# Streamed tiles of an expert kernel at other distances from the loaded tiles, a first column per region, and two capacities raised by 4 and 2

## The chip, the core and the metric

The kernel runs on one core of one Trainium2 chip. The metric is the device time of one execution in microseconds, the median of several runs. A core has five engines with queues of their own: TensorE (PE, matrix products; its loads of stationary blocks are listed as PEld), VectorE (DVE), ScalarE (ACT), GpSimd (POOL) and SyncE (SP, which issues most DMA here). SBUF is the on-chip memory of 128 partitions; the products write to PSUM.

## What is computed

Linear attention with a normalisation, then a two-level mixture of experts over its rows, all in float32:

```python
kv = np.einsum('bhsd,bhse->bhde', k, v)
out = np.einsum('bhsd,bhde->bhse', q, kv)
rms = np.sqrt(np.mean(out * out, axis=-1, keepdims=True) + 1e-06)
x = (out / rms * g_norm)                  # as 4608 rows of 512
g_idx = argmax(x @ w_group); g_w = its softmax
for g in range(4):                        # groups
    e_idx = argmax(x[g_idx == g] @ w_expert[g]); e_w = its softmax
    for e in range(4):                    # experts of the group
        h = np.maximum(x_ge @ w1[g, e], 0.0)       # 512 -> 1024
        out[tok_idx] = (g_w * e_w)[:, None] * (h @ w2[g, e])   # 1024 -> 512
```

## The kernel before

**First phase** (to about 158 us). q, k and v are loaded, the attention and the router's decisions are computed, the rows go to a table in DRAM (scr), and the sixteen experts are ranked by their number of rows. The expert of rank 0 is computed largely in this phase. Its products are in plain f32.

**Second phase** (from 158.58 us). A loop over r = 1 to 15 takes the experts in the order of their rank. Each such pass is called a region here. CAPS[r] is the number of row slots that the region has (rows beyond it go to a loop at the end that runs only when it is needed). For a region, GpSimd gathers the rows (xg), they go through DRAM (xd) and come back turned (xq, xt), and ACT and DVE split them into a rounded part xh and a rest xl, both in float32r, a float32 type for the products. The expert's weights come as four pieces of 1 MB (wr) and are split in the same way into whi and wlo. The results go through DRAM (yd) back to rows, and GpSimd scatters them.

A product is then three: high by high, rest by high, high by rest. That is the helper `three` (lines 306 to 316): for each chunk of the inner dimension, line 310 streams the high part against the loaded whi, line 311 streams the rest against whi, and line 315 streams the high part against wlo (in the code's order of the three). Layer 1 (`layer1`) has 8 output blocks x 4 chunks x 3 = 96 such products, streaming xh and xl; its result goes through `split_h` (lines 284 and 285) into hh and hl. Layer 2 (`layer2_by_feature`) has 4 blocks x 8 chunks x 3 = 96, streaming hh and hl. So a region has 192 products, each with CAPS[r] columns that are streamed and a block of 128 x 128 that is loaded. Only in the last region's layer 2 (`layer2_by_token`) are the roles swapped: hh and hl are loaded, and the weights are streamed in 256 columns.

The places in SBUF: the pool `cp` lies first, then `big` (twelve slots of 8 KB, tag w8, with all whi and wlo), then the tiles of the second phase (pool `mp`), among them xg, xq, xt, xh, xl, yo, hh and hl in this order. The tiles xh, xl, hh and hl are 384 columns wide per chunk (1,536 bytes a partition); a region uses the first CAPS[r] of them.

The order of the second phase is written out by hand (`manual_schedule`): each engine runs its instructions in the order of the code.

Of the kernel before, what the change touches and what calls it, by code (L numbers as in the profile page):

```python
# [9 lines left out]
F32 = mybir.dt.float32  # L10
F32R = mybir.dt.float32r
# [7 lines left out]

CAPS = [384, 364, 354, 330, 326, 312, 302, 300, 292, 290, 284, 274, 268, 264, 260, 256]


GS = [8, 7, 5, 5, 7, 4]
# [32 lines left out]
def tile_linattn_moe(ctx: ExitStack, tc: tile.TileContext, qm, qt, k, v, router, w1, w2, out):  # L58
    nc = tc.nc
    P = 128  # L60
# [16 lines left out]
    KC = DM // P  # L77
    FC = FF // P
# [7 lines left out]
    RW = DM + H  # L86
# [2 lines left out]
    yd = [tc.dram_tile([3 * P, DM], F32, name=f"yd{i}") for i in range(2)]  # L89
    ovt = tc.dram_tile([NBLK, 4], F32, name="ovt")  # L90

    cp = ctx.enter_context(tc.tile_pool(name="cp", bufs=1))
    big = ctx.enter_context(tc.tile_pool(name="big", bufs=BIG))


# [61 lines left out]
    for r in range(NE):  # L157
        nc.gpsimd.memset(caps[:, r:r + 1], float(CAPS[r]))
    blk = cp.tile([P, 36], F32, name="blk")
# [83 lines left out]
    def split_piece(w, p, turned=False):  # L243
        for x, hi, lo in quarter(w, p, turned):
            nc.scalar.copy(out=hi, in_=x)  # L245
            nc.vector.tensor_tensor(out=lo, in0=x, in1=hi.bitcast(F32), op=ALU.subtract)  # L246

    def blocks(cap):
        return [(j, min(P, cap - j * P)) for j in range((cap + P - 1) // P)]

    def gather_rows(xg, rows, idx, src=scr):
        return nc.gpsimd.indirect_dma_start(out=xg[0:rows, 0:RW], out_offset=None, in_=src,  # L252
                                            in_offset=bass.IndirectOffsetOnAxis(ap=idx[0:rows, :], axis=0))
# [20 lines left out]
    def scale_rows(eng, xg, out_=None):  # L274

        x = by_quarter(xg[:, 0:DM])
        out_ = x if out_ is None else by_chunk(out_)
        for h in range(2):
            hs = slice(2 * h, 2 * h + 2)
            d = eng.tensor_tensor(out=out_[:, hs], in0=x[:, hs], in1=factors(xg)[:, h], op=ALU.mult)  # L280
        return d

    def split_h(hh, hl, ps):
        nc.scalar.activation(out=hh, in_=ps, func=AF.Relu)  # L284
        nc.vector.scalar_tensor_tensor(out=hl, in0=ps, scalar=0.0, in1=hh.bitcast(F32), op0=ALU.max, op1=ALU.subtract)  # L285

    def layer1(ps, w1, f, xh, xl):
        cs = slice((f % 4) * P, (f % 4 + 1) * P)
        _, wh, wl = w1[f // 4]
        three(ps, KC, lambda c: wh[:, c, cs], lambda c: wl[:, c, cs], lambda c: xh[:, c, :], lambda c: xl[:, c, :])  # L290
# [846 lines left out]
    with ExitStack() as ph:  # L1137
        mp = ph.enter_context(tc.tile_pool(name="moe", bufs=2))
# [87 lines left out]
        def quarter_rows(x, cap, a):  # L1226
            n = (cap + 31) // 32
            return x[0:32 * n, a * P:(a + 1) * P].rearrange("(b i) f -> i b f", i=32)

        def gather(r):  # L1230
            xg = mp.tile([P, 3, RW], F32, name="xg", bufs=1)
            for j, _ in blocks(CAPS[r]):
                st["gather"] = gather_rows(xg[:, j], P, gidx[:, r, j:j + 1])
            return xg

        def scale(r, g):
            for j, _ in blocks(CAPS[r]):
                scale_rows(nc.gpsimd, g[:, j])

        def put_x(r, g):  # L1240
            for j, rows in blocks(CAPS[r] + -CAPS[r] % 32):
                nc.sync.dma_start(xd[r % 2][j * P:j * P + rows, :], g[0:rows, j, 0:DM])

        def get_x(r):
            n = (CAPS[r] + 31) // 32
            xq = mp.tile([P, 12, P], F32, name="xq", bufs=1)
            for a in range(4):
                nc.sync.dma_start(xq[32 * a:32 * a + 32, 0:n, :], quarter_rows(xd[r % 2], CAPS[r], a))
            return xq, mp.tile([P, KC, 384], F32, name="xt", bufs=1)
# [3 lines left out]
            nc.vector.transpose(out=xt[:, c, 0:32 * n].rearrange("p (b i) -> p b i", i=32),  # L1253
                                in_=xq[:, 0:n, 32 * c:32 * c + 32])

        def parts_x():
            return [mp.tile([P, KC, 384], F32R, name=nm, bufs=1) for nm in ("xh", "xl")]

        def split_x(r, parts, xt, c):

# [5 lines left out]
        def put_y(r, yq):  # L1266
            for a in range(4):
                nc.sync.dma_start(quarter_rows(yd[r % 2], CAPS[r], a), yq[32 * a:32 * a + 32, 0:(CAPS[r] + 31) // 32, :])

        def get_y(r, yq):  # L1270
            yo = mp.tile([P, 3 * DM], F32, name="yo3", tag="yo3").rearrange("p (j f) -> p j f", j=3)
            for j, rows in blocks(CAPS[r]):
                nc.sync.dma_start(yo[0:rows, j], yd[r % 2][j * P:j * P + rows, :])
            return [(yo[:, j], rows, gidx[:, r, j:j + 1]) for j, rows in blocks(CAPS[r])]

        def back(r, yt):

            yo = mp.tile([P, 3 * DM], F32, name="yo3", tag="yo3").rearrange("p (j f) -> p j f", j=3)
            for j, rows in blocks(CAPS[r]):
                tp = ps_t.tile([P, 512], F32, name="tp2", tag="pst")  # L1280
                for d in range(KC):
                    nc.tensor.transpose(tp[0:rows, d * P:(d + 1) * P], yt[:, d, j * P:j * P + rows], ident)
                nc.vector.tensor_copy(out=yo[0:rows, j], in_=tp[0:rows, :])
                scatter_rows(yo[:, j], rows, gidx[:, r, j:j + 1])
                yield
# [46 lines left out]
        nxt = gather(1)  # L1332
# [19 lines left out]
        for i in range(2, 4):  # L1352
            load_next(i)
        nxt = gather(2)
        scale(2, nxt)
        for c in range(KC):
# [8 lines left out]
        for hf in range(2):  # L1365
# [1 line left out]
            for f in range(4):  # L1367
                whole1(ps[:, f * P:(f + 1) * P], w1c[hf][:, :, f * P:(f + 1) * P], xT)
            nc.scalar.activation(out=hT[:, 4 * hf:4 * hf + 4], in_=ps.rearrange("p (f t) -> p f t", f=4), func=AF.Relu)
        cur = parts_x()  # L1370
        for c in range(KC):
            turn_x(1, xq, xt, c)
        for c in range(KC):
# [16 lines left out]
        for r in range(1, NE):  # L1390
            cap = CAPS[r]
            xh, xl = cur
            hh = mp.tile([P, FC, 384], F32R, name="hh", bufs=1)
            hl = mp.tile([P, FC, 384], F32R, name="hl", tag="hl", bufs=1)
            if nxt:
                xq, xt = get_x(r + 1)
            if todo and todo[0] in MOVED:
                put_y(*todo)
            elif todo:
                turns = back(*todo)  # L1400
            for f in range(FC):
                if f in w2_at:
                    split_piece(w2c, w2_at[f], r in MOVED)
                ps = ps_h.tile([P, 512], F32, name="ps")
                layer1(ps[:, 0:cap], w1c, f, xh[:, :, 0:cap], xl[:, :, 0:cap])
                split_h(hh[:, f, 0:cap], hl[:, f, 0:cap], ps[:, 0:cap])
                if r > 1:
                    next(tables, None)
                    next(tables, None)
                elif f < len(psys):  # L1410
                    nc.vector.memset(psys[f][:, DM // 2:384], 0.0)
                if f == 0:
                    nxt2 = gather(r + 2) if r + 2 < NE else None
                if nxt2 and f == 1:
                    scale(r + 2, nxt2)
                if f >= 1:
                    next(turns, None)
                if todo and todo[0] in MOVED and f == 2:
                    results = get_y(*todo)
                if nxt and f in (1, 3):  # L1420
                    load_next((f + 3) // 2)
                if nxt2 and f == 4:
                    put_x(r + 2, nxt2)
                if f >= 5 and results:
                    scatter_rows(*results.pop(0))
                if f == FC - 1 and r + 1 == NE:
                    nc.gpsimd.drain()
            nw1a, nw2a, load_a = weight_loads(eidx[0:1, r + 2:r + 3], mp if r % 2 else None) if nxt2 else (None, None, None)
            cur = parts_x() if nxt else None

            def side(n, total, after):
                if nxt is None:
                    return
                if not after:
                    split_piece(nw1, n)
                    if n < 2:
                        turn_x(r + 1, xq, xt, 2 * n)
                        turn_x(r + 1, xq, xt, 2 * n + 1)
                else:
                    for c in ([0], [1, 2], [3], [])[n]:  # L1440
                        split_x(r + 1, cur, xt, c)
                    if n in (1, 3) and nxt2:
                        load_a(n // 2)

            if r + 1 == NE:
                layer2_by_token(r, w2c, hh, hl, side)
            else:
                todo = layer2_by_feature(r, w2c, hh, hl, side)
            w1c, w2c = nw1, nw2
            nxt, nw1, nw2, load_next = nxt2, nw1a, nw2a, load_a  # L1450
# [3 lines left out]
    with ExitStack() as ph:  # L1454
# [4 lines left out]
        with tc.For_i(0, nv, 1) as it:  # L1459
# [19 lines left out]
            xg = op.tile([P, RW], F32, name="xgo")  # L1479
# [90 lines left out]
```

## Time and profile before

| | us |
|---|---|
| median of 3 runs | 567.9 (567.41 to 568.88) |
| profiled execution | 565.66 |
| its span, first to last instruction | 564.0 |
| PE busy | 543.9 (96%) |
| DVE / ACT / POOL busy | 378.1 / 267.1 / 209.3 |
| mean granted clock of TensorE | 0.991 |

The profile is of one execution. A row of a cut (a stretch of the span) gives its start and end, its length, the busy time of each engine in it with the number of instructions that touch it, the granted clock as a share of 2.4 GHz, and the share of the DMA engines' time with the rate. Products are pipelined: one starts well before the one ahead of it has ended, so what a product costs is the time between starts, not its duration.

### The profile page before, as it was taken

How to read it: one execution, taken by the hardware profiler on the slowest of the kernel's cores; microseconds unless marked ns; L12 is line 12 of the kernel's file. 1: busy time of each engine (PE TensorE's matmuls, PEld its weight loads, DVE VectorE, ACT ScalarE, POOL GpSimd, SP SyncE). 2: the span in 40 equal slices, each digit the busy share in tenths (PEclk: the TensorE clock that was granted, in tenths of full speed). 3: DMA queues.
4: the chain of work that ended last, by engine and by line, in shares of the span. 5: the costliest groups of instructions: out<-in, count | busy, mean ns of one | idle time of the engine just before them, and what ended most of it. 6: DMA issues, size and time to landing. Idle time of an engine off the chain costs nothing.

```text
span 564.0 us, 11522 instructions
## 1 busy us (share of the span) xinstructions
PE 543.9 (96%) x4323; PEld 522.6 (93%) x4323; DVE 378.1 (67%) x782; ACT 267.1 (47%) x530; POOL 209.3 (37%) x278
## 2 busy tenths in 40 slices
PE   8999978699899999999999999999999999999995
PEld 3899868588899999999999999999999999999995
DVE  4247888773456796776767676777767686868750
ACT  0377754622444443544444544454546455546540
POOL 5024342144352342533453524344525334433121
PEclk9999998899999999999999999999999999999998
DMA  8999999486889999999998999999999999989940
GB/s 286 388 407 388 370 355 405 126 316 229 281 318 299 283 311 261 274 307 283 309 293 288 281 291 261 320 278 332 313 300 294 292 309 315 319 254 331 271 144 34
DMA packets 78890, 165.21 MB, mean 293 GB/s; under 512 B 8084, under 2 KB 47332, under 8 KB 67824
## 3 DMA queue, kind: packets, MB, share of 16 engines
q1 hardware_dynamic: 70862, 142.29, 78.7%
q0 software_dynamic: 7824, 22.11, 13.1%
q8 instruction: 35, 0.57, 0.4%
q10 hardware_dynamic: 146, 0.04, 0.1%
q14 instruction: 23, 0.19, 0.1%
HBM read 126.38 MB, written 38.55 MB: 292 GB/s over the span
## 4 chain that ended last, share of the span: by engine, by line
PE 69%; DMA 19%; issue 5%; DVE 2%; SPq 2%; ACT 2%; POOL 1%; POOLq 0%; DVEq 0%; ACTq 0%
PE ps L311 8%; PE ps L315 8%; PE ps L310 8%; DMA wr<-in_w_dram 8%; PE psy L311 8%; PE psy L310 8%; PE psy L315 8%; PE ops L515 5%; PE kps L477 3%; PE l L299 3%; PE warm L371 3%; DMA yd<-yq 2%; DMA xd<-xg 2%; DMA xq<-xd 2%; DMA ktail<-in_k_dram 2%
## 5 line engine op out<-in xcount | busy, mean ns | idle before, releaser
L246 DVE TENSOR_TENSOR wlo<-wr,whi 128x1024 fp32r<-128x1024 f32 (+1 forms) x176 | 156.6, 917 | 22.6 <-ACT whi L245 19.1
L311 PE MATMUL ps<-xl,whi 128*128 128x364 f32 (+14 forms) x480 | 144.5, 301 | 0.0
L315 PE MATMUL ps<-xh,wlo 128*128 128x364 f32 (+14 forms) x480 | 144.4, 301 | 0.0
L310 PE MATMUL ps<-xh,whi 128*128 128x364 f32 (+14 forms) x480 | 144.4, 301 | 0.0
L311 PE MATMUL psy<-hl,whi 128*128 128x364 f32 (+13 forms) x448 | 135.5, 302 | 0.0
L315 PE MATMUL psy<-hh,wlo 128*128 128x364 f32 (+13 forms) x448 | 135.4, 302 | 0.0
L310 PE MATMUL psy<-hh,whi 128*128 128x364 f32 (+13 forms) x448 | 135.2, 302 | 0.0
L245 ACT CAST whi<-wr 128x1024 fp32r<-128x1024 f32 (+1 forms) x176 | 128.2, 769 | 1.9 <-DMA wr<-in_w_dram 1.9
L284 ACT ACTIVATE hh<-ps 128x364 fp32r<-128x364 f32 (+14 forms) x120 | 50.4, 420 | 146.8 <-PE ps L315 142.4
L285 DVE SCALAR_TENSOR_TENSOR hl<-ps,hh 128x364 fp32r<-128x364 f32 (+14 forms) x120 | 55.8, 465 | 56.9 <-ACT hh L284 55.2
L310 PEld LDWEIGHTS ps<-xh,whi 128*128 128x128 f32 x480 | 90.8, 189 | 0.0
L315 PEld LDWEIGHTS ps<-xh,wlo 128*128 128x128 f32 x480 | 90.7, 189 | 0.0
L311 PEld LDWEIGHTS ps<-xl,whi 128*128 128x128 f32 x480 | 90.5, 189 | 0.0
L252 POOL DMA_INDIRECT xg<-scr,gall x44 | 52.6, 1196 | 96.2 <-DMA xd<-xg 81.2
L280 POOL TENSOR_TENSOR xg<-xg 128x256 f32<-128x256 f32 x82 | 60.2, 762 | 74.5 <-DMA xg<-scr,gall 74.4
L256 POOL DMA_INDIRECT out_dram<-yo,gall x45 | 51.8, 1150 | 92.8 <-DMA yo<-yd 75.9
L310 PEld LDWEIGHTS psy<-hh,whi 128*128 128x128 f32 x448 | 84.7, 189 | 0.0
L315 PEld LDWEIGHTS psy<-hh,wlo 128*128 128x128 f32 x448 | 84.7, 189 | 0.0
L311 PEld LDWEIGHTS psy<-hl,whi 128*128 128x128 f32 x448 | 84.5, 189 | 0.0
L1262 ACT ACTIVATE xh<-xt,rw 128x364 fp32r<-128x364 f32 (+14 forms) x60 | 32.3, 543 | 48.5 <-DVE xt L1253 45.5
L1315 DVE STREAM_TRANSPOSE yq<-psy 128x320 f32<-128x320 f32 (+3 forms) x56 | 28.5, 510 | 29.9 <-PE psy L315 27.6
L515 PE MATMUL ops<-kvx,m_q 128*128 128x168 f32 x256 | 42.0, 312 | 0.6 <-ACT xr L466 0.6
(250 smaller groups left out, 588.7 us busy)
## 6 DMA issues: line engine op xcount, KB each, us to landing
wr<-in_w_dram SPq DMA_DIRECT2D x64, 1024.0 KB
scr<-xo SPq DMA_DIRECT2D x36, 256.0 KB
m_q<-in_qm_dram SPq DMA_DIRECT2D x8, 1024.0 KB
xd<-xg SPq DMA_DIRECT2D x32, 256.0 KB
m_k<-in_k_dram SPq DMA_DIRECT2D x7, 1024.0 KB
m_v<-in_v_dram SPq DMA_DIRECT2D x7, 1024.0 KB
yo<-yd SPq DMA_DIRECT2D x28, 256.0 KB
xq<-xd SPq DMA_DIRECT2D x20, 160.0 KB
```

Of the source, the lines that this page charges most:

```text
L245: nc.scalar.copy(out=hi, in_=x)
L246: nc.vector.tensor_tensor(out=lo, in0=x, in1=hi.bitcast(F32), op=ALU.subtract)
L252: return nc.gpsimd.indirect_dma_start(out=xg[0:rows, 0:RW], out_offset=None, in_=src, in_offset=bass.IndirectOffsetOnAxis(ap=idx[0:rows, : ...
L256: sc = nc.gpsimd.indirect_dma_start(out=out, out_offset=bass.IndirectOffsetOnAxis(ap=idx[0:rows, :], axis=0), in_=yo[0:rows, :], in_offset ...
L280: d = eng.tensor_tensor(out=out_[:, hs], in0=x[:, hs], in1=factors(xg)[:, h], op=ALU.mult)
L284: nc.scalar.activation(out=hh, in_=ps, func=AF.Relu)
L285: nc.vector.scalar_tensor_tensor(out=hl, in0=ps, scalar=0.0, in1=hh.bitcast(F32), op0=ALU.max, op1=ALU.subtract)
L310: nc.tensor.matmul(ps, lhsT=stat_h(c), rhs=mov_h(c), start=(c == 0), stop=False)
L311: nc.tensor.matmul(ps, lhsT=stat_h(c), rhs=mov_l(c), start=False, stop=False)
L315: nc.tensor.matmul(ps, lhsT=stat_l(d), rhs=mov_h(d), start=False, stop=(d == n - 1))
L515: nc.tensor.matmul(o, lhsT=raw["q", b].rearrange("p j f -> p (j f)")[:, (pr * NJ + j) * P:(pr * NJ + j + 1) * P], rhs=kvx[b % 4][:, pr], s ...
L1262: nc.scalar.activation(out=xh, in_=x, func=AF.Copy, scale=g2[:, 0:1])
```

## The change

Four things change. A tile of 8 float32 columns (32 bytes a partition) named gap is put at the head of `cp`; nothing reads or writes it. The tile xg gets 24 columns (96 bytes) more at its end. A table BEGIN gives for each region the first column that it uses in xh, xl, hh and hl, and a helper `streamed` cuts the tiles accordingly. CAPS[4] goes from 326 to 330 and CAPS[9] from 290 to 292.

```diff
-CAPS = [384, 364, 354, 330, 326, 312, 302, 300, 292, 290, 284, 274, 268, 264, 260, 256]
+CAPS = [384, 364, 354, 330, 330, 312, 302, 300, 292, 292, 284, 274, 268, 264, 260, 256]
+
+BEGIN = [0, 16, 16, 0, 0, 0, 0, 0, 40, 40, 8, 0, 40, 0, 16, 0]
...
     cp = ctx.enter_context(tc.tile_pool(name="cp", bufs=1))
+    cp.tile([P, 8], F32, name="gap")
...
         def gather(r):
-            xg = mp.tile([P, 3, RW], F32, name="xg", bufs=1)
+
+            xg = mp.tile([P, 3 * RW + 24], F32, name="xg", bufs=1)[:, 0:3 * RW].rearrange("p (j f) -> p j f", j=3)
...
-        def parts_x():
-            return [mp.tile([P, KC, 384], F32R, name=nm, bufs=1) for nm in ("xh", "xl")]
+        def streamed(r, nm, n=KC):
+            return mp.tile([P, n, 384], F32R, name=nm, bufs=1)[:, :, BEGIN[r]:BEGIN[r] + CAPS[r]]
+
+        def parts_x(r):
+            return [streamed(r, nm) for nm in ("xh", "xl")]
...
-            hh = mp.tile([P, FC, 384], F32R, name="hh", bufs=1)
-            hl = mp.tile([P, FC, 384], F32R, name="hl", tag="hl", bufs=1)
+            hh, hl = (streamed(r, nm, FC) for nm in ("hh", "hl"))
...
-            cur = parts_x() if nxt else None
+            cur = parts_x(r + 1) if nxt else None
```

The program's instructions stay the same in number and order on every engine.

## Rows read from the trace of the kernel before

**Rows 1.** The page: busy time by engine, and the chain that ended last

```profile
PE 543.9 (96%) x4323; PEld 522.6 (93%) x4323; DVE 378.1 (67%) x782; ACT 267.1 (47%) x530; POOL 209.3 (37%) x278
...
PE 69%; DMA 19%; issue 5%; DVE 2%; SPq 2%; ACT 2%; POOL 1%; POOLq 0%; DVEq 0%; ACTq 0%
```

**Rows 2.** Second phase cut at the starts of regions 1 to 15, busy by engine

```profile
core 0: us, PE busy (x) PEld busy (x) DVE busy (x) ACT busy (x) POOL busy (x), PEclk, DMA share, GB/s
158.58:190.86 32.28, 32.28 (x194) 32.25 (x193) 20.25 (x34) 15.26 (x27) 13.28 (x15) 1.00 1.00 307
190.86:222.85 31.99, 31.99 (x194) 31.99 (x193) 25.29 (x48) 13.69 (x24) 11.43 (x12) 1.00 1.01 285
222.85:252.29 29.44, 29.44 (x193) 29.44 (x193) 21.95 (x48) 13.52 (x24) 11.62 (x14) 1.00 0.95 289
252.29:281.42 29.13, 29.13 (x195) 29.13 (x194) 20.21 (x40) 13.45 (x24) 10.81 (x11) 1.00 1.01 290
281.42:309.15 27.73, 27.73 (x194) 27.73 (x193) 19.41 (x32) 13.34 (x24) 11.42 (x12) 1.00 0.93 292
309.15:336.03 26.88, 26.88 (x195) 26.88 (x193) 19.71 (x32) 13.26 (x24) 12.26 (x12) 1.00 1.02 294
336.03:362.90 26.87, 26.87 (x194) 26.87 (x193) 19.18 (x32) 13.21 (x24) 10.64 (x11) 1.00 0.99 293
362.90:388.31 25.41, 25.41 (x195) 25.41 (x194) 18.52 (x32) 13.15 (x24) 10.49 (x11) 1.00 1.01 300
388.31:414.54 26.23, 26.23 (x194) 26.23 (x193) 19.20 (x32) 13.11 (x24) 11.68 (x12) 1.00 1.02 320
414.54:440.15 25.61, 25.61 (x195) 25.61 (x193) 18.67 (x32) 13.03 (x24) 10.48 (x11) 1.00 0.98 288
440.15:464.68 24.53, 24.53 (x195) 24.53 (x193) 18.39 (x32) 12.95 (x24) 10.62 (x12) 1.00 0.97 281
464.68:488.15 23.47, 23.47 (x195) 23.47 (x194) 18.24 (x32) 12.90 (x24) 11.84 (x12) 1.00 0.98 298
488.15:511.50 23.35, 23.35 (x194) 23.35 (x193) 16.64 (x32) 12.47 (x24) 7.51 (x8) 1.00 0.91 294
511.50:534.56 23.06, 23.06 (x195) 23.06 (x194) 17.37 (x34) 12.77 (x24) 4.54 (x5) 1.00 0.99 305
534.56:557.62 23.06, 23.06 (x194) 22.86 (x192) 9.45 (x15) 7.34 (x15) 5.58 (x6) 1.00 0.36 118
sum 399.04, PE 399.04 PEld 398.81 DVE 282.50 ACT 193.43 POOL 154.22; mean PE 26.60 PEld 26.59 DVE 18.83 ACT 12.90 POOL 10.28
```

**Rows 3.** Chain that ended last, first phase: start, us, what, number of products

```profile
25.10 1.14 PE ops L515 x8
...
33.91 1.14 PE ops L515 x8
...
44.05 1.14 PE ops L515 x8
```

**Rows 4.** Idle time ahead of the instructions that read wr: us, times

```profile
  DMA wr<-in_w_dram: 1.9, 2
```

**Rows 5.** Timeline at region 15's start, DVE and PE: start, us, instruction

```profile
534.19 0.44 DVE L1263 SCALAR_TENSOR_TENSOR xl<-xt,rw,xh 128x256 fp32r<-128x256 f32 x1
...
534.56 0.28 PE L310 MATMUL ps<-xh,whi 128*128 128x256 f32 x1
...
535.75 0.28 PE L311 MATMUL ps<-xl,whi 128*128 128x256 f32 x1
```

**Rows 6.** The first 100 us as one cut, columns as in rows 2

```profile
0.00:100.00 100.00, 92.25 (x1141) 78.79 (x1142) 62.92 (x184) 52.13 (x132) 33.25 (x87) 0.98 1.00 371
```

More of the change, by code (lines that the diff above doesn't have):

```diff
@@ L1369, in tile_linattn_moe @@
             nc.scalar.activation(out=hT[:, 4 * hf:4 * hf + 4], in_=ps.rearrange("p (f t) -> p f t", f=4), func=AF.Relu)
-        cur = parts_x()
+        cur = parts_x(1)
         for c in range(KC):
```

## Prediction

> **What bounds the kernel now.** I read the page first: TensorE (PE) is busy 96% of the span, VectorE (DVE) 67%, and the chain that ended last lies 69% on PE [rows 1]. A share of busy time does not say where, so next comes the second phase cut at the starts of its fifteen regions r = 1 to 15 [rows 2]. In every cut PE is busy for the whole length and the granted clock is 1.00, the 2.4 GHz level. The reader should take from this table only its first two numbers: the 192 products of a region follow each other without a gap, so a region's length over 192 is the time from one product's start to the next. The phase is 399.0 of the 564.0 us, and it is the sum of 2880 such steps.
>
> For bookkeeping I count one streamed column as one period of 2.4 GHz, 0.417 ns. A region of 292 columns then owes 121.7 ns a product and takes 25.41/192 = 132.3: an excess of 10.7 ns. By region, from CAPS and [rows 2], the excess is 16.5 (364 columns, the phase's first gap in it), 19.1 (354), 15.8 (330), 15.9 (326), 14.4 (312), 14.2 (302), 14.9 (300), 10.7 (292), 15.8 (290), 15.1 (284), 13.6 (274), 10.6 (268), 11.6 (264), 11.8 (260), 13.4 (256, the last product's tail in it). All columns together are 4476 x 192 x 0.417 ns = 358.1 us; the excess is 40.9 us. That is what the change can act on.
>
> Two things about this excess count. It does not follow the number of columns: 290 columns take 136.6 ns and 292 take 132.3; 302 and 300 both take 140.0; 268 take 0.6 ns more than 264 and 274 take 5.6 more than 268. So it is not a slower column, but something that depends on how a product's stream of bytes comes to lie against something else. What runs beside it is the load of the next product's stationary block, which reads SBUF at the same time and just as densely: PEld is as busy as PE [rows 2]. And in the first phase, where plain f32 products of 168 columns spend two periods a column, eight take 1.14 us, 142.5 ns each against 140.0 owed: 2.5 ns of excess [rows 3]. There the streamed windows of kvx begin 160 bytes apart, and in the program as built the three stretches have twelve different distances between the streamed tile and the loaded one (m_q); they cost the same. So at half the reading rate no distance costs anything, and at the full rate of the second phase something does.
>
> **The change, part by part.** The program issues the same instructions in the same order on all engines; only addresses and a few widths differ. The distance below is the address of the first streamed column less that of the first loaded one, modulo 512 bytes: the steps between chunks are multiples of 512 on both sides, so one number holds for a region. As built it is 96 bytes before, for all products but the last 96 (the second layer of r = 15, where the roles are swapped: 416).
>
> Gap and pad. The gap tile moves everything in SBUF by 32 bytes, the pad of xg moves the streamed tiles by 96 more. No instruction, no time of their own. The distance becomes 192. What DMA writes moves too; all tiles still begin on multiples of 32 bytes, and tiles on odd and on even multiples were both in use before. I take 0; were DMA slower by 1% in the first 100 us, where its share is 1.00 [rows 6], that would be 1 us, and I keep it inside the range.
>
> First columns. BEGIN adds 64 bytes at r = 1, 2, 14 (distance 256), 160 at r = 8, 9, 12 (352), 32 at r = 10 (224). No row shows a product at 192, 224, 256, 320 or 352. If the pattern repeats every 256 bytes, 352 is 96 again and r = 8 and 12, the two cheapest regions, stay as they are. I assume that; if it repeats only every 512 they join the unknown ones, with the same bounds.
>
> Capacities. r = 4 goes from 326 to 330 columns: 192 x 4 x 0.417 ns = 0.32 us, and the row of 330 against that of 326 says the same at the old distance, 29.44 - 29.13 = 0.31. r = 9 goes from 290 to 292: by the two rows 25.41 - 26.23 = -0.82 us. On ACT and DVE some 24 instructions each of those regions get 4 or 2 columns of 300 longer, about 1%; DVE has 27 to 31% idle there and ACT half, which hides it. Uncovered it would be 0.1 us. Six more rows of 2 KB are stored and fetched, out of 165 MB.
>
> The unknown is the excess of the twelve regions at new distances (r = 1 to 7, 10, 11, 13 to 15). Their excesses add up to 176 ns, 176 x 192 = 33.9 us, a mean of 14.7 ns. From below it is bounded by the 2.5 ns of the plain products [rows 3]: 5.8 us, a gain of 28. From above by the worst region, 19.1 ns [rows 2]: 44.0 us, a loss of 10.1. I take 10.6 ns, the level at which the two cheapest regions of this same instruction stand; it is the nearest row to what a good distance gives, since it is the only one at the full reading rate. 12 x 192 x 10.6 ns = 24.4 us, a gain of 9.5. With +0.3 and -0.8 the sum is -10.0 us.
>
> The Trainium skill speaks against any effect: "SBUF — State Buffer", section "Who interferes with whom", gives PE two read ports, one for the streamed operand and one for the weight load, and says that PE never waits on anyone; "TensorE: Matmul & The Clock Gate", section "Back-to-back issue gap", puts a warm product at its columns over 2.4 GHz plus 2.5 ns. The plain products agree with it to the digit. By it the second phase would take 358.1 + 2880 x 2.5 ns = 365.3 us; the trace has 399.0, so for these products the rule leaves 34 us open.
>
> What is late next. The profiled execution took 565.7 us (span 564.0); the runs' median is 567.9, 2.2 above. I apply the difference to both: a span of 554, a median of 557.9. Ten us off 376 (to the last region's start) shorten a region by 0.7 us. What has to keep up is DMA, whose share is 0.91 to 1.02 in these cuts [rows 2], though packets of two queues overlap in it. The weights already came late twice, 1.9 us of ACT's time [rows 4], but ACT is half idle. The tightest margin that I found is the last piece of xl before r = 15: DVE ends it at 534.63, and PE, which starts the region at 534.56, first reads it at 535.75 [rows 5], 1.1 us later. It shrinks, but does not close by 0.7 us. I take no give-back in the likeliest case.
>
> **The rivals.**
>
> (1) The distance does not matter; the excess comes from widths alone. For: the twelve distances of [rows 3]. Against: 290 columns are dearer than 292, which a port to itself does not explain. Then only the capacities act, +0.3 - 0.8: 567.4. The rule of the Trainium skill weighed above is this case.
>
> (2) The feed takes the gain back. For: DMA shares near 1.00, and cuts that are 9 us shorter now than at the start with the same 4 MB of weights each. If the mean share of about 0.985 over 376 us is real, only 1.5%, 5.6 us, is there to win: 562.3. Against: PE did not wait once, and the first 100 us moved 371 GB/s [rows 6] against about 295 here. PE would show idle time before the first product of late regions.
>
> (3) The new distances collide more. The streams still run at once; where the loaded block's bytes fall in step with the streamed ones for longer, each product pays more. At the level of the worst row, 19.1 ns, in twelve regions: +10.1 + 0.3 - 0.8 = +9.6, 577.5. It decides from a mean of 14.9 ns in those regions, just 0.2 above today's, so only the level tells. For: nothing in the trace has tried these distances. Against: 96 is not a good one for these widths, 14.7 on average, and there is more room below (to 10.6 and 2.5) than above (to 19.1); the two regions with the least to win keep their distance modulo 256.
>
> (4) The excess nearly goes, towards 2.5 ns. That is 28 us of PE's time, of which the feed lets through perhaps half: around 550.
>
> **How the numbers follow.** The likeliest case, 10 us off, gets 0.58, with 549 to 563 as its own range; (1) 0.12, (2) 0.13, (3) 0.12, (4) 0.05. Faster by over 0.3% (1.7 us, about what a measurement of this kernel can tell from no change) are the likeliest, (2) and (4): 0.76; within it (1): 0.12; slower (3): 0.12. The range leaves out (3) and part of (4): 549 to 568.5. The predicted time is 557.9 us.
>
> **What would show it.** Cut at region starts, the profile after should have regions near columns x 0.417 + 10.6 ns: 30.4 us for 354 columns in place of 31.99, 28.4 for 330 in both r = 3 and 4, 26.2 for 302. r = 8, 9 and 12 should read 25.4, 25.4 and 23.5. PE should still have no idle time. I am wrong if r = 3 and 4 stay at 29.4 (rival 1), if idle PE time appears before r = 10 to 15 (rival 2), if most regions lengthen (rival 3), or if r = 8 and 12 move by more than 0.3 us (the pattern does not repeat at 256).

## The result, and the profile after

The changed kernel took 563.21 us, the median of four runs (561.19 to 565.53), beside 568.39 for the kernel before, measured with it (567.41 to 571.98): the medians are 5.2 us apart. The ratio on record is 0.9895, with an interval of 0.9856 to 0.9934: 6.0 us less, between 3.8 and 8.2. A second set of six runs gave 562.42 and the ratio 0.9895 again. The forecast of "faster" and its range held; the gain was forecast at 10 us and came out at about 6.

Before the rows, a warning on what is compared. The profiled execution of the changed kernel took 565.53 us (span 563.8), the longest of its four. The one of before took 565.66, shorter than each of the four runs above. So these two profiles lie beside each other with nearly the same time, and only a cut by region shows what has changed. The cut below is the second phase of the changed kernel at the starts of its fifteen regions, columns as in [rows 2].

```profile
159.75:191.95 32.20, 32.20 (x195) 32.17 (x193) 20.22 (x34) 15.26 (x27) 13.38 (x16) 1.00 0.98 304
191.95:222.68 30.73, 30.73 (x194) 30.73 (x193) 24.87 (x48) 13.71 (x24) 12.19 (x13) 1.00 1.02 296
222.68:252.44 29.76, 29.76 (x195) 29.76 (x193) 23.20 (x48) 13.54 (x24) 13.52 (x16) 1.00 0.99 304
252.44:282.20 29.76, 29.76 (x194) 29.76 (x193) 20.59 (x40) 13.48 (x24) 9.54 (x9) 1.00 1.00 287
282.20:309.59 27.39, 27.39 (x193) 27.39 (x193) 19.41 (x32) 13.33 (x24) 12.11 (x12) 1.00 0.88 274
309.59:336.05 26.46, 26.46 (x194) 26.46 (x193) 18.91 (x32) 13.26 (x24) 11.23 (x12) 1.00 1.03 306
336.05:362.30 26.25, 26.25 (x194) 26.25 (x193) 19.80 (x32) 13.21 (x24) 10.85 (x11) 1.00 0.94 299
362.30:387.69 25.39, 25.39 (x194) 25.39 (x193) 19.22 (x32) 13.16 (x24) 8.87 (x10) 1.00 0.99 285
387.69:413.08 25.39, 25.39 (x194) 25.39 (x193) 19.15 (x32) 13.13 (x24) 11.16 (x12) 1.00 0.96 287
413.08:438.16 25.08, 25.08 (x194) 25.08 (x193) 18.97 (x32) 13.05 (x24) 12.92 (x12) 1.00 0.98 302
438.16:462.49 24.33, 24.33 (x194) 24.33 (x193) 18.14 (x32) 12.96 (x24) 12.14 (x12) 1.00 0.98 295
462.49:485.96 23.47, 23.47 (x195) 23.47 (x193) 16.33 (x29) 11.58 (x22) 8.55 (x11) 1.00 0.95 294
485.96:510.66 24.70, 23.39 (x194) 23.18 (x193) 16.16 (x32) 11.50 (x23) 7.21 (x9) 1.00 1.01 299
510.66:534.73 24.07, 23.06 (x195) 22.85 (x193) 19.03 (x35) 14.68 (x28) 4.95 (x5) 1.00 0.98 315
534.73:557.51 22.78, 22.78 (x194) 22.57 (x192) 9.80 (x16) 7.75 (x15) 6.29 (x6) 1.00 0.38 120
sum 397.76, PE 395.44 PEld 394.79 DVE 283.81 ACT 193.59 POOL 154.91; mean PE 26.36 PEld 26.32 DVE 18.92 ACT 12.91 POOL 10.33
```

Three things differ from [rows 2]. Most regions are shorter: r = 2 by 1.26 us (31.99 to 30.73), r = 7 by 0.62, r = 9 by 0.84 (this one by its new capacity), r = 10 by 0.53. The two regions of 330 columns, r = 3 and 4, are longer, at 29.76 where 330 columns took 29.44 before. And in r = 13 and 14 the busy time of PE (second number) falls short of the length (first) by 1.31 and 1.01 us: PE waits, which it did nowhere before. The waits of PE in this phase are two. The rows give us in total, times, and the longest.

```profile
PE psy L314 <- DVE yq L1323: 1.3, 1, 1.3
PE ps L315 <- DVE xl L1271: 1.0, 1, 1.0
```

PE waits once for DVE to empty a PSUM tile (yq) and once for DVE to make a piece of xl. DVE itself waited for transfers, by its own rows of the same trace:

```profile
DVE xt L1258 <- DMA xq<-xd: 13.2, 5, 5.2
...
DVE yq L1323 <- DMA yd<-yq: 3.8, 3, 2.3
```

In the trace of before the first of these was shorter:

```profile
DVE xt L1253 <- DMA xq<-xd: 8.3, 4, 3.6
```

The page, as [rows 1]: PE's busy time went from 543.9 to 541.0 us, and its share of the chain that ended last from 69 to 74%.

```profile
PE 541.0 (96%) x4315; PEld 520.2 (92%) x4323; DVE 379.5 (67%) x782; ACT 267.5 (47%) x530; POOL 210.3 (37%) x278
...
PE 74%; DMA 17%; issue 4%; POOL 1%; DVE 1%; ACT 1%; SPq 0%; POOLq 0%; DVEq 0%
```

### The profile page after: what moved, and what is told of

Same layout as the page of the kernel before. It is cut to its first block, busy times and chain, and to the rows that moved or that the text cites. A ratio compares the mean times of both kernels' runs of the same rounds, so it can differ in the third digit from the quotient of the medians.

```text
span 563.8 us, 11514 instructions
## 1 busy us (share of the span) xinstructions
PE 541.0 (96%) x4315; PEld 520.2 (92%) x4323; DVE 379.5 (67%) x782; ACT 267.5 (47%) x530; POOL 210.3 (37%) x278
## 3 DMA queue, kind: packets, MB, share of 16 engines
q0 software_dynamic: 7968, 22.11, 12.9%
## 4 chain that ended last, share of the span: by engine, by line
PE 74%; DMA 17%; issue 4%; POOL 1%; DVE 1%; ACT 1%; SPq 0%; POOLq 0%; DVEq 0%
PE ps L315 10%; PE ps L319 10%; PE ps L314 10%; PE psy L315 10%; PE psy L314 10%; PE psy L319 10%; DMA wr<-in_w_dram 5%; PE ops L519 4%; PE l L303 3%; DMA m_q<-in_qm_dram 3%; DMA m_k<-in_k_dram 3%; PE kps L481 2%; DMA ktail<-in_k_dram 2%; DMA m_v<-in_v_dram 2%; DMA yd<-yq 2%
## 5 line engine op out<-in xcount | busy, mean ns | idle before, releaser
L315 PE MATMUL ps<-xl,whi 128*128 128x330 f32 (+12 forms) x480 | 144.0, 300 | 1.0 <-DVE xl L1271 1.0
L314 PE MATMUL ps<-xh,whi 128*128 128x330 f32 (+12 forms) x480 | 143.8, 300 | 0.0
L319 PE MATMUL ps<-xh,wlo 128*128 128x330 f32 (+12 forms) x480 | 143.7, 299 | 0.0
L314 PE MATMUL psy<-hh,whi 128*128 128x330 f32 (+11 forms) x448 | 134.8, 301 | 1.3 <-DVE yq L1323 1.3
L315 PE MATMUL psy<-hl,whi 128*128 128x330 f32 (+11 forms) x448 | 134.8, 301 | 0.0
L319 PE MATMUL psy<-hh,wlo 128*128 128x330 f32 (+11 forms) x448 | 134.6, 301 | 0.0
L288 ACT ACTIVATE hh<-ps 128x330 fp32r<-128x330 f32 (+12 forms) x120 | 50.5, 421 | 136.7 <-PE ps L319 131.6
L289 DVE SCALAR_TENSOR_TENSOR hl<-ps,hh 128x330 fp32r<-128x330 f32 (+12 forms) x120 | 55.5, 465 | 50.7 <-ACT hh L288 47.9
L256 POOL DMA_INDIRECT xg<-scr,gall x44 | 49.1, 1115 | 90.9 <-DMA xd<-xg 69.2
L1270 ACT ACTIVATE xh<-xt,rw 128x330 fp32r<-128x330 f32 (+12 forms) x60 | 32.3, 543 | 56.1 <-DVE xt L1258 54.8
L1323 DVE STREAM_TRANSPOSE yq<-psy 128x320 f32<-128x320 f32 (+3 forms) x56 | 28.4, 506 | 28.5 <-PE psy L319 24.5
```

The lines of the kernel that those rows point to most:

```text
L314: nc.tensor.matmul(ps, lhsT=stat_h(c), rhs=mov_h(c), start=(c == 0), stop=False)
L315: nc.tensor.matmul(ps, lhsT=stat_h(c), rhs=mov_l(c), start=False, stop=False)
L319: nc.tensor.matmul(ps, lhsT=stat_l(d), rhs=mov_h(d), start=False, stop=(d == n - 1))
L1270: nc.scalar.activation(out=xh, in_=x, func=AF.Copy, scale=g2[:, 0:1])
```

## The experiments

Excess below means what the prediction meant: the time between starts of two products less 0.417 ns a column. The theory to be tested is that a product's excess is set by its columns and by the distance of its streamed from its loaded tile, modulo 256 bytes. Against it stand the place of the tiles as such (gap and pad move everything), the capacities, and the feed, which may give back what PE gains. What had to be explained besides is why 330 columns came out dearer.

**Four kernels that scan the distance.** Each takes the capacities of before and BEGIN = 0 throughout, and shifts the tiles so that layer 1 runs at one distance and layer 2 at another. So one run prices two distances for all widths. Against the changed kernel, besides the capacities:

```diff
-BEGIN = [0, 16, 16, 0, 0, 0, 0, 0, 40, 40, 8, 0, 40, 0, 16, 0]
+BEGIN = [0] * 16
...
-            xg = mp.tile([P, 3 * RW + 24], F32, name="xg", bufs=1)[:, 0:3 * RW].rearrange("p (j f) -> p j f", j=3)
+            xg = mp.tile([P, 3 * RW + 40], F32, name="xg", bufs=1)[:, 0:3 * RW].rearrange("p (j f) -> p j f", j=3)
...
+            if r == 1:
+                mp.tile([P, 8], F32, name="gap2", bufs=1)
             hh, hl = (streamed(r, nm, FC) for nm in ("hh", "hl"))
```

That is distance 0 for layer 1 and 32 for layer 2. For 64 and 128 the two numbers 40 and 8 are 56 and 16, for 160 and 224 they are 80 and 16. For 192 and 208 the pad stays at 24 and hh and hl begin at their column 4.

> All regions at one distance: layer 1 at 0 bytes (modulo 256), layer 2 at 32; capacities of before. Theory (columns and distance modulo 256 together set the time of a product): the two layers of a region differ from each other and from before's; at 0 bytes layer 1 of 354 columns repeats the 15.37 us and of 260 columns the 11.39 us that they take in the changed kernel. Rival (the tiles' absolute places, or the slack of the feed, set it): these do not repeat, or both layers of a region stay alike. I expect layers between 10.6 and 19.1 ns of excess a product.

> Layer 1 of all regions at 64 bytes, layer 2 at 128. Theory: excess between 10.6 and 19.1 ns by columns, with another order of cheap and dear widths than at 96; the last layer of the last region (loaded and streamed swapped) changes as well. Rival: both layers alike.

> Layer 1 at 160 bytes, layer 2 at 224. Theory: layer 2 of 284 columns repeats the 12.54 us that it takes at 224 in the changed kernel; others unknown, 10.6 to 19.1 ns of excess. Rival: it stays at before's 12.80.

> Layer 1 at 192 bytes, layer 2 at 208, that is half a step of 32 further. Theory: layer 1 repeats the changed kernel's 14.88 (330 columns), 13.71 (312), 13.23 (302), 13.13 (300), 12.17 (274), 11.55 us (264). If steps under 32 bytes matter, layer 2 differs from layer 1; if the pattern has steps of 32, layer 2 is like 192 or like 224 (12.54 at 284 columns).

Measured, one execution each: 562.89, 568.23, 565.99 and 565.83 us, beside 568.06 for before. The second phase took 395.0, 397.9, 396.7 and 396.6 us (399.0 before). Cut at the layers, the lengths over 96 give the excess. Two rows of layer 2 with 354 columns, at distance 32 (first kernel) and at 128 (second):

```profile
207.51:222.87 15.36, 15.36 (x97) 15.36 (x97) 11.35 (x21) 7.34 (x11) 6.09 (x5) 1.00 1.04 320
```

```profile
209.70:225.39 15.69, 15.69 (x99) 15.69 (x97) 12.44 (x22) 7.36 (x11) 8.85 (x9) 1.00 0.99 310
```

15.36/96 = 160.0 ns, an excess of 12.5, and 15.69/96 = 163.4, an excess of 15.9. At 96, as before, it was 19.1. For eight of the widths, worked out in this way, to about 0.1 (ns; 96 from the regions of before, 192 from this scan and other runs; a second number where a later run of this study came out otherwise at the same distance):

| columns | 0 | 32 | 64 | 96 | 128 | 160 | 192 | 224 |
|---|---|---|---|---|---|---|---|---|
| 354 | 12.5 | 12.6 | 12.5 | 19.1 | 15.8 | 12.6 | 19.0 | 14.2 |
| 330 | 12.5, 15.8 | 13.6 | 15.8 | 15.8 | 15.8 | 12.6 | 11.4, 17.5 | 15.8 |
| 312 | 12.8 | 13.4 | 12.2 | 14.4 | 10.1, 16.7 | 14.0 | 12.7 | 13.3 |
| 302 | 11.9 | 12.9 | 14.2 | 14.2 | 14.2 | 11.1 | 12.0, 14.2 | 14.2 |
| 292 | 11.7 | 11.7 | 10.4 | 10.6 | 10.0 | 11.7 | 11.7 | 11.7 |
| 290 | 12.5 | 12.5 | 12.5 | 15.8 | 12.5 | 15.6 | 15.1 | 13.8 |
| 284 | 15.0 | 11.7, 12.8 | 12.0 | 15.0, 12.8 | 13.4 | 15.0 | 15.0 | 12.3 |
| 274 | 12.5, 15.8 | 12.5 | 12.5 | 13.6 | 12.6 | 14.7 | 12.5 | 13.3 |

Most of the lengths that had been expected to repeat did, to 0.02 us: 354 and 260 columns at 0, 284 at 224, and 312, 300, 274 and 264 at 192. 330 and 302 at 192 did not. What follows: the distance matters (rival 1 falls), and each width has its own best distance in this scan, so a table per region seemed to have a use. But no distance is good for all: over the fourteen widths from 364 to 260 the mean in the scan is 12.5 at 0, 12.6 at 64 (without the stretches in which PE waited), 13.5 at 192 with its cheap numbers, and 14.2 at 96. 10.6 ns, the level of the two cheapest regions of before, is reached by single widths and is not what a good distance gives in general. Not even steps of 16 bytes are alike: at 192 (layer 1) and 208 (layer 2) 330 columns differ by 0.26 us in 96 products, in the one execution of the fourth kernel.

```profile
225.23:239.53 14.30, 14.30 (x98) 14.30 (x97) 11.17 (x30) 6.22 (x13) 5.21 (x6) 1.00 0.87 252
239.53:254.09 14.56, 14.56 (x98) 14.56 (x97) 11.14 (x18) 7.32 (x11) 7.46 (x10) 1.00 0.98 333
```

14.30/96 = 149.0 ns for 330 columns at 192. The changed kernel had 29.76/192 = 155.0 at that same distance. That contradicts the theory as it stood and led to the next run.

**The changed kernel once more**, with nothing but a comment added.

> The changed kernel, unaltered, once more. Two kernels gave regions of 330 columns, at the same addresses, 155.0 and 148.9 ns a product. Theory A (a product's time has several steady patterns, and which one a region falls into hangs on the state in which it is entered, so it may differ between executions): some regions come out at another length than 29.76 us (330), 26.46 (302), 27.40 (312), 22.78 (256) while all addresses are the same; 28.6 us for 330 columns would be the other pattern. Theory B (widths, addresses and the order of instructions fix it): all regions repeat to 0.1 us except where PE sits idle. Feed theory: idle PE time of 0 to 4 us, in regions 12 to 15, where VectorE waits for yd or xq; timed 1% below before.

562.42 us in the median (560.51 to 566.33), ratio 0.9895 (0.9854 to 0.9935). Its profiled execution took 560.51, the shortest of the six, 5 us less than the first profile of the same program. Its cut, columns as above:

```profile
223.82:252.40 28.58, 28.58 (x193) 28.58 (x193) 22.29 (x48) 13.53 (x24) 12.58 (x14) 1.00 1.00 313
252.40:280.99 28.59, 28.59 (x194) 28.59 (x193) 20.95 (x40) 13.48 (x24) 10.45 (x10) 1.00 1.04 296
...
507.81:530.60 22.79, 22.79 (x195) 22.79 (x193) 18.02 (x35) 13.52 (x26) 4.07 (x4) 1.00 1.02 329
530.60:552.54 21.94, 21.94 (x194) 21.74 (x192) 9.47 (x15) 7.41 (x15) 5.91 (x6) 1.00 0.38 118
sum 391.63, PE 391.63 PEld 391.41 DVE 282.98 ACT 193.63 POOL 154.11; mean PE 26.11 PEld 26.09 DVE 18.87 ACT 12.91 POOL 10.27
```

PE waits nowhere, r = 3 and 4 take 28.58 and 28.59 us in place of 29.76, r = 15 takes 21.94 in place of 22.78, and the other regions are the same to 0.02 us except for the two in which PE had waited. It is one program at one set of addresses. The difference stands in the starts of single products. PE's timeline in r = 3, start and duration in us, first in the first profile of the changed kernel:

```profile
229.81 0.31 PE L315 MATMUL ps<-xl,whi 128*128 128x330 f32 x1
...
230.43 0.31 PE L319 MATMUL ps<-xh,wlo 128*128 128x330 f32 x1
...
230.89 0.32 PE L319 MATMUL ps<-xh,wlo 128*128 128x330 f32 x1
```

and products of the same kind in the second:

```profile
229.77 0.31 PE L315 MATMUL ps<-xl,whi 128*128 128x330 f32 x1
...
230.37 0.31 PE L319 MATMUL ps<-xh,wlo 128*128 128x330 f32 x1
...
230.81 0.31 PE L319 MATMUL ps<-xh,wlo 128*128 128x330 f32 x1
```

Seven steps take 1.08 us (154 ns each) in the one and 1.04 (149) in the other. Both hold for the whole region (29.76/192 = 155.0 and 28.58/192 = 148.9), at the granted clock of 1.00. So the same products can run in more than one steady pattern, and an execution falls into one of them; the longer one is called the dear pattern below. The runs of this study were made on several chips, but the chip does not decide it: on the chip of this second profile the distances alone (below) had 29.76 us for r = 3, and on another one 28.59 came without the gap and 29.76 with a second buffer.

**The capacities alone**, on the kernel before:

```diff
-CAPS = [384, 364, 354, 330, 326, 312, 302, 300, 292, 290, 284, 274, 268, 264, 260, 256]
+CAPS = [384, 364, 354, 330, 330, 312, 302, 300, 292, 292, 284, 274, 268, 264, 260, 256]
```

> Capacities 330 and 292 alone, all else as before, distance 96. r = 4 29.44 us (+0.31), r = 9 25.40 (-0.83), the other regions as before to 0.1 us under theory B; under theory A one or two may differ. Time -0.5 us, 0.1%, not to be told from before.

567.67 us (565.24 to 573.53), ratio 0.9998 (0.9968 to 1.0028). r = 4 and r = 9 in the cut:

```profile
252.94:282.38 29.44, 29.44 (x195) 29.44 (x193) 20.04 (x40) 13.48 (x24) 9.28 (x10) 1.00 1.02 286
...
389.27:414.66 25.39, 25.39 (x195) 25.39 (x193) 19.43 (x32) 13.13 (x24) 8.83 (x10) 1.00 0.96 277
```

+0.31 and -0.84 us against [rows 2], both terms of the sum as they were worked out, and together too little for a measurement to show.

**The distances alone**: the changed kernel with the capacities of before.

```diff
-CAPS = [384, 364, 354, 330, 330, 312, 302, 300, 292, 292, 284, 274, 268, 264, 260, 256]
+CAPS = [384, 364, 354, 330, 326, 312, 302, 300, 292, 290, 284, 274, 268, 264, 260, 256]
```

> The changed kernel with capacities 326 and 290. From the scan, 326 columns at 192 take 150.0 ns: r = 4 28.8 us in place of 29.76; 290 at 352 as at 96: 26.23 in place of 25.39. Sum as in the changed kernel to 0.2 us, 0.9 to 1% below before. If the capacities carried the gain, it would stand at before's time.

562.91 us, ratio 0.9896 (0.986 to 0.9932), which is the changed kernel's. The gain is the distances'. PE waits nowhere in its profile. Its r = 3, 4 and 9:

```profile
224.57:254.33 29.76, 29.76 (x194) 29.76 (x193) 22.49 (x48) 13.52 (x24) 11.50 (x14) 1.00 0.96 294
254.33:283.13 28.80, 28.80 (x194) 28.80 (x193) 20.29 (x40) 13.44 (x24) 10.43 (x10) 1.00 1.01 298
...
388.63:414.87 26.24, 26.24 (x195) 26.24 (x193) 19.59 (x32) 13.10 (x24) 11.65 (x11) 1.00 0.97 299
```

r = 3 fell into the dear pattern here as well, and r = 4 came at the 28.8 us expected. r = 9, with 290 columns at distance 352, takes 26.24 us; at 96 it took 26.23. So for this pair of distances, 96 and 352, the price repeats after 256 bytes. One other pair 256 apart was run: 284 columns at 480, listed as 224 in the scan, took 12.56 us a layer, and 12.54 at 224 in the changed kernel.

**A table from the scan.** The first columns are chosen by the four scans, on a base distance of 0, with 326 and 292 columns for r = 4 and 9:

```diff
-CAPS = [384, 364, 354, 330, 330, 312, 302, 300, 292, 292, 284, 274, 268, 264, 260, 256]
+CAPS = [384, 364, 354, 330, 326, 312, 302, 300, 292, 292, 284, 274, 268, 264, 260, 256]
-BEGIN = [0, 16, 16, 0, 0, 0, 0, 0, 40, 40, 8, 0, 40, 0, 16, 0]
+BEGIN = [0, 16, 0, 0, 0, 32, 0, 0, 32, 32, 8, 0, 24, 16, 0, 40]
...
-            xg = mp.tile([P, 3 * RW + 24], F32, name="xg", bufs=1)[:, 0:3 * RW].rearrange("p (j f) -> p j f", j=3)
+            xg = mp.tile([P, 3 * RW + 40], F32, name="xg", bufs=1)[:, 0:3 * RW].rearrange("p (j f) -> p j f", j=3)
```

> Each region at the distance that was cheapest for its width in the scan: 64 (364 columns), 0 (354, 330, 326), 128 (312), 0 (302, 300), 128 (292 in both r = 8 and 9), 32 (284), 0 (274), 96 (268), 64 (264), 0 (260), 160 (256). Excess a product by the scan 13.3, 12.5, 12.5, 13.1, 10.1, 11.9, 11.7, 10.0, 10.0, 11.7, 12.5, 10.5, 10.6, 10.3, 10.6 ns: 33.0 us in all, 7.9 below before and 4 below the changed kernel. Theory B: the phase takes 391.5 us plus idle time. Theory A: some regions fall into dearer patterns. Feed theory: the idle PE time grows with the gain; the time falls by 4 to 8 us, 0.7 to 1.4%.

563.57 us (562.26 to 564.63), ratio 0.9897 (0.9863 to 0.993): no better than the changed kernel. Its second phase took 396.8 us in the profile, where 391.5 and idle time had been expected. r = 3 and r = 14 of its profile:

```profile
222.41:251.85 29.44, 29.44 (x195) 29.44 (x194) 22.00 (x48) 13.51 (x24) 10.88 (x12) 1.00 0.98 298
...
508.41:533.24 24.83, 23.33 (x194) 22.91 (x193) 17.91 (x34) 13.40 (x27) 4.83 (x4) 1.00 0.95 293
```

330 columns at distance 0 had an excess of 12.5 in layer 1 of the scan, 150.0 ns a product; here 29.44/192 = 153.3. A price taken from one execution did not carry over to the next. And in r = 14 PE waits 1.5 us, busy 23.33 of 24.83.

**The gap alone**, on the kernel before, and **the changed kernel without it**:

```diff
     cp = ctx.enter_context(tc.tile_pool(name="cp", bufs=1))
+    cp.tile([P, 8], F32, name="gap")
```

```diff
     cp = ctx.enter_context(tc.tile_pool(name="cp", bufs=1))
-    cp.tile([P, 8], F32, name="gap")
```

> Before, with the 32-byte tile gap alone: every tile 32 bytes on, all distances as before. The six kernels with the gap start the second phase at 159.8 to 162.3 us, the two without it at 158.6 and 159.2. Theory G (the shift itself costs something in the first phase): second phase from 160 to 161.5 us, its regions as before (31.99 at 354, 29.44 at 330, 25.40 at 292), time +1.5 to 2 us (0.3%). Rival (chance between executions): start at 158.6 to 159.5, time as before within 0.2%.

> The changed kernel without the gap: distances the same, all places in SBUF 32 bytes back. Theory (the distance counts, not the place): regions as in the changed kernel, 30.73 (354), 25.40 (292), 25.08 (284), 22.79 (260), and 330 columns at 29.76 or 28.59. If the place of the streamed or the loaded tile counts by itself, these move. Theory G: the second phase starts at 158.6 to 159.3 and the time is 1.5 to 2 us under the changed kernel, about 561; rival: no difference to it.

The gap alone: 568.27 us, ratio 0.9997 (0.9978 to 1.0016). Without it: 562.44, ratio 0.9897 (0.9859 to 0.9935), as with it. All fifteen regions of the first kernel are those of before to 0.02 us; r = 1 and 2:

```profile
164.57:196.85 32.28, 32.28 (x195) 32.25 (x193) 19.92 (x34) 15.26 (x27) 12.94 (x15) 1.00 0.97 307
196.85:228.84 31.99, 31.99 (x194) 31.99 (x193) 25.15 (x48) 13.70 (x24) 13.05 (x15) 1.00 1.00 300
```

Those of the second are the ones of the changed kernel's second profile, also to 0.02 us, but for r = 14, which is 0.65 us longer (23.44); r = 2 and the sum:

```profile
192.59:223.32 30.73, 30.73 (x194) 30.73 (x193) 24.84 (x48) 13.70 (x24) 12.14 (x13) 1.00 0.99 295
...
sum 392.29, PE 392.17 PEld 391.53 DVE 281.43 ACT 193.29 POOL 150.56; mean PE 26.14 PEld 26.10 DVE 18.76 ACT 12.89 POOL 10.04
```

All tiles lie 32 bytes further on or back, streamed and loaded alike, and the lengths stay, while 32 bytes of distance changed them in the scan. So the distance counts and not the place. The profiled execution of the gap alone shows something else: its second phase begins at 164.57 us, 6 later than in before, in a run of 571.7 us, the longest of its twelve. The five profiles without the gap start the second phase at 158.6 to 160.4 us, the nine with it at 159.8 to 164.6. That the gap has a part in this is not excluded by one profile each, but the time shows none: the medians are 568.27 and 568.29, and the interval leaves at most 0.9 us of loss.

**A second buffer for yq.** One of PE's waits went back to DVE waiting for yd, a transfer out of yq. Here yq gets two buffers, and xT shares the slots of yo to make room:

```diff
-            yq = mp.tile([P, 12, P], F32, name="yq", tag="yq", bufs=1)
+            yq = mp.tile([P, 12, P], F32, name="yq", tag="yq", bufs=2)
...
-        xT = mp.tile([P, KC, P], F32, name="xT", bufs=1)
-        hT = mp.tile([P, 12, P], F32, name="hT", tag="yq", bufs=1)[:, 0:FC]
+        xT = mp.tile([P, KC, P], F32, name="xT", tag="yo", bufs=2)
+        hT = mp.tile([P, 12, P], F32, name="hT", tag="yq", bufs=2)[:, 0:FC]
```

The gap is left out as in the kernel ahead. The first kernel keeps the table of the change, the second takes

```diff
-CAPS = [384, 364, 354, 330, 330, 312, 302, 300, 292, 292, 284, 274, 268, 264, 260, 256]
+CAPS = [384, 364, 354, 330, 326, 312, 302, 300, 292, 292, 284, 274, 268, 264, 260, 256]
-BEGIN = [0, 16, 16, 0, 0, 0, 0, 0, 40, 40, 8, 0, 40, 0, 16, 0]
+BEGIN = [0, 16, 16, 0, 0, 48, 0, 0, 48, 48, 8, 0, 40, 0, 16, 0]
```

> As no_gap, and two buffers for yq (xT shares the place of yo, to make room). In the changed kernel VectorE waited 3.8 us for yd<-yq to free the one buffer, and PE once for VectorE. Feed theory: with two buffers those waits go, idle PE time falls to what xq still causes; 0 to 2 us under no_gap. Rival (the feed as a whole is short, the wait moves to xq or wr): same idle time, same time as no_gap.

> As no_gap_yq2, with 312 columns at distance 128 (26.92 us in place of 27.40), 292 at 128 (25.29 for 25.40, twice) and capacity 326 at 192 in r = 4 (28.80 for 28.59 or 29.76). By these lengths 0.5 to 1.7 us under no_gap_yq2, at about 559.5; as the fed-back idle time grows it may be half of that.

With the table of the change: 563.76 us (561.79 to 565.32), ratio 0.9906 (0.9875 to 0.9937), no better than without the buffer. DVE's wait for yd is gone from the trace, but PE waits all the same, twice, and DVE's wait for xq is 15.7 us (11.1 without the second buffer):

```profile
PE ps L314 <- DVE xl L1270: 1.2, 1, 1.2
PE ps L313 <- DVE hl L288: 1.0, 1, 1.0
```

```profile
DVE xt L1257 <- DMA xq<-xd: 15.7, 6, 4.4
```

With the other table: 562.06 us (559.32 to 569.5), ratio 0.9882 (0.9844 to 0.992). This is the lowest median of the study, but its interval overlaps that of the changed kernel, and no claim is made for it. PE waited nowhere in its profile, and its second phase took 392.8 us. Of its regions r = 5, moved to distance 128 for the 10.1 ns of the scan, shows the same as the table ahead:

```profile
279.82:307.98 28.16, 28.16 (x195) 28.16 (x194) 18.99 (x32) 13.32 (x24) 12.34 (x14) 1.00 0.87 285
```

28.16/192 = 146.7 ns, an excess of 16.7, where the table ahead had 26.92 us for these columns at this distance, an excess of 10.2. The distance that had the lowest price for 312 columns in the scan had the highest one here.

## Why the prediction was right, and where its size was off

**What bounds the kernel: held.** The second phase went by the starts of its products, in every profile, and each kernel whose distances changed had other region lengths with the same columns. Rival 1 is out: with only addresses moved, 354 columns went from 31.99 to 30.73 us, and that length came back in all seven profiles that have r = 2 at this distance, within 0.01 us. The rule in the Trainium skill, "SBUF — State Buffer", section "Who interferes with whom", that PE's two read ports are independent and PE waits for no one, does not describe these products: at the same granted clock of 1.00 the same instructions differ by up to 6.6 ns each with the distance alone. Of the other page of the Trainium skill that it weighed, "TensorE: Matmul & The Clock Gate", section "Back-to-back issue gap", the prediction left out that the section calls the gap of columns over 2.4 GHz plus 2.5 ns that of an isolated product, and has the spacing in a stream of loads and products set by both. The 34 us that the prediction found left open are of such a stream. What it is that collides was not measured; that the loading of the next block is the other party is argued from the distance being the thing that counts.

**No cost of gap and pad: held** for the gap, between 1.3 us faster and 0.9 us slower (0.9978 to 1.0016). The pad was not tried apart; it is what makes the distance.

**Repeat at 256 bytes: held** where it was tried. r = 8 and 12 at distance 352 read 25.39 and 23.47 us against 25.41 and 23.47 at 96, and 290 columns 26.24 against 26.23.

**The capacities: held** at the old distance, +0.31 and -0.84 against +0.3 and -0.8. At the new distance of r = 4 the term does not stand by itself, since 330 columns at 192 took 28.59 or 29.76 us and 326 took 28.80. Without the two capacities the kernel is as fast, 562.91.

**The excess of the twelve regions: mis-sized.** This is the step that failed. It set 10.6 ns in place of 14.7, a gain of 9.5 us. In the best of the profiles, the second one of the changed kernel, the whole phase went from 399.04 to 391.63, 7.41 less; 0.84 of that is r = 9, 0.02 r = 8 and 12, and r = 4 has four columns more (0.32). So the twelve gained 7.41 - 0.84 - 0.02 + 0.32 = 6.9 us, 3.0 ns a product, to a mean of 11.7. The prediction took the two cheapest of fifteen regions for the level of a good distance. The scan shows that those stand near the low end of a scatter: by distance, the mean over the widths is 12.5 ns at best.

**No give-back: failed, in part of the executions.** The first profile of the changed kernel kept only 1.28 us of the 7.41. The rest was lost to the dear pattern, 1.18 and 1.17 us in r = 3 and 4 and 0.84 in r = 15, and to r = 13 and 14, 24.70 - 23.07 + 24.07 - 22.79 = 2.9 us, of which 2.3 are PE's waits. These five make 6.1. Rival 2 had named the sign, idle time ahead of late regions, and it appeared: in the first profile, in the scan with 64 and 128, with the scan's table and with the second buffer, and by 0.1 us without the gap. It did not appear in the second profile of the same program, nor with the distances alone. The prediction had named xl at the start of r = 15 as the tightest margin, 1.1 us [rows 5]; the piece that came late was an xl, of r = 14. A second buffer removed DVE's wait for yd, and PE waited in that profile all the same, so it is not this one buffer; that the feed as a whole is short there is the likely reading and was not shown. That the waits depend on the execution was seen, and why was not.

**From profile to median: too simple.** The prediction set the median 2.2 us above the profiled time in both kernels. The first profile of the changed kernel lies 2.3 above its median, the second 1.9 below. The three profiles of the changed distances and capacities with one buffer have phases of 397.8, 391.6 and 392.3 us, a mean of 393.9, which is 5.1 below before, near the 6.0 of the ratio.

**What the range was worth.** 563.2 us lies in the stated range, but so does the time of before, 568.39; it was the direction that was at stake. Within the range 563.2 is just above the likeliest case's own part (549 to 563) and near the price of rival 2 (562.3). That nearness is luck: rival 2 got there by a ceiling of the feed that leaves 5.6 us to win, and in the second profile, where PE never waits, the phase alone is 7.4 us shorter.

**What would show it.** 30.4 us had been named for 354 columns (30.73 came), 28.4 for 330 (28.58, or 29.76 in the dear pattern), 26.2 for 302 (26.46), 25.4, 25.4 and 23.5 for r = 8, 9 and 12 (25.39, 25.39, 23.47). Of the forecast's own signs for an error, r = 3 and 4 not below 29.4 was there in the first profile and would have spoken for rival 1; the second profile shows that it was no sign of that.

## What to carry to other kernels

When products follow each other without a gap and still take longer than their columns, compare regions of nearly equal width: a step that does not follow the width points to addresses, and moving the first column of a tile by some tens of bytes is a cheap trial. Take for a forecast the mean of what such places cost and not the best one, because the best one seen is partly luck. And before a choice among places is made from one profile, profile the same program twice: if region lengths differ between executions, a table drawn from single runs will not hold.

## What was not expected of the hardware

The same program at the same addresses has more than one steady time for a product: 148.9 or 155.0 ns for 330 columns at distance 192, at the granted clock of 1.00. In r = 3 each keeps to one from its first dozen of products (1.79 or 1.86 us) to its last. 312 columns at 128 took 140.2 or 146.7 ns in two programs that have this distance. It is not the new distances' doing: 284 columns at 96 took 25.61 us in before [rows 2] and 25.17 with the capacities alone, where nothing in that region differs:

```profile
414.66:439.83 25.17, 25.17 (x194) 25.17 (x193) 19.04 (x32) 13.05 (x24) 11.04 (x12) 1.00 0.99 301
```

What decides at the entry of a region stays open.

These times are not spread evenly. Counted in periods of 0.417 ns, the regions of [rows 2] over 192 are 399.9 for 354 columns, 368.0 for 330, 336.0 for 302, 335.9 for 300, 327.9 for 290 and 320.1 for 284: multiples of 8 to within 0.2. Most others stand at halves or thirds of such a step (364.1 for 326, 346.6 for 312, 293.4 for 268), and so do the two patterns of 330 columns at 192 (372.0 and 357.3). That is how 302 and 300 columns can cost the same; what sets the steps was not looked into.

The granted clock of the scan at 160 and 224 read 0.95 throughout its second phase, and its products took no longer for it. 284 columns in layer 2, at 224 modulo 256, took 12.56 us there:

```profile
427.80:440.36 12.56, 12.56 (x99) 12.56 (x98) 9.81 (x17) 7.11 (x11) 4.71 (x4) 0.95 0.89 298
```

In the changed kernel both layers of r = 10 have these columns at this distance, at 1.00, and took 25.08 us, 12.54 each. So a record of 0.95 did not mean slower products here.
